# Batches 0 and 1 share the first layer by halves of its columns, and 1/sqrt is cut in two

## The chip, the core and the metric

The kernel runs on one core of a Trainium2 chip. The metric is the device time of one execution in microseconds (us); three runs of the kernel before gave a median of 1693.56 us (1692.34 to 1693.83). TensorE (PE) multiplies matrices, VectorE (DVE), ScalarE (ACT) and GpSimd (POOL) do elementwise work, and SyncE (SP) issues most DMAs. Every engine works through its own list of instructions in order; semaphores make one engine wait for another.

## The reference, cut to what matters

```
phi_w = softmax(phi, axis=seq) ; k_m = phi_w^T k ; v_m = phi_w^T v      # 8 batches, 8 heads, 576 tokens, 32 memories
x  = softmax(q k_m^T / 8) v_m                                            # -> 4608 tokens x 512
xn = x / sqrt(mean(x*x) + 1e-6) * rms_g
y  = (silu(xn @ w_gate) * (xn @ w_val)) @ w_out                          # 512 -> 1536 -> 512, float64 weights
out = (relu(y @ w_in2) ** 2) @ w_out2                                    # 512 -> 2048 -> 512
```

The weights arrive as 64-bit floats. The kernel turns each 128x512 piece of them into float32 on the core by integer work (a *conversion*), and splits every factor of the big products into a high and a low part, so that three matmuls make one product.

## The kernel before, in words

**Phase A** computes attention and the first layer (gate, val, out). A batch has 576 tokens, worked on in two halves of 288. The first layer's 1536 columns are cut into NF1 = 12 groups of 128. One *item* is one half of a batch's tokens with one column group: `phase_a` runs six matmuls for g (L748 to L750), Silu on ACT (L786), six matmuls for v, the product `sl` on DVE (L790), its high part `uh` on ACT and low part `ul` on POOL (the helper `split`, L68 and L72), and two items later twelve matmuls into the four accumulators y (`mm_out`, L762 to L764). A batch has 24 items, item n belongs to batch n // 24; there are 192. After the last column group of a half, y goes to `st` and by DMA to DRAM (L769 to L772). **Phase B** then runs the second layer from DRAM.

Into these items other work is put at four places, "a" to "d": after g, after v, after `split`, after `mm_out`. A table in `make_plan` says at which item of batch b which step of the attention of batch b+1 ("n") or b+2 ("p") is issued, and `slot` calls it. Steps that the prediction names: `p1` to `p7` (softmax of phi), `t1`, `a3` (k_m and v_m), `a7` to `a9` (scores), `a10` to `a15` (softmax), `a18`, `a19` and `sq_add` (x and its squares), `a20` (their sum), `a21` (1/sqrt by nine DVE operations, L467 to L475), `a23`, `an_split` (high and low part of x for the matmuls). The weights gate and val are folded with each batch's v_m: `wp_mm` (L504, PE) and `wp_ev` make the factors `wph`, `wpl` for two column groups at once, a *chunk*; there are six.

**Conversions.** `conv_next` starts one conversion (two ACT operations, L102 and L103) and ends the one started before: two DVE operations (L111, L112), an integer add on POOL (L116), for a piece of w_out ("o") also the high part `woh` on ACT and the low part `wol` on POOL, and then the next raw DMA (`next_raw`, four buffers). The first layer needs 36 conversions: 24 of gate and val ("g", "v", four for each chunk) and 12 of "o". The prologue, which computes batch 0's attention, calls `conv_next` five times; then `slot` calls it three times in each of items 0 to 11, since batch 0 takes the column groups in order and needs a new chunk every second item:

```
        if b == 0 and i < NF1 and pos in "abc":
            self.conv_next()
```

In PSUM there are one buffer for g, one for v, two for attention and four for y. The tiles of the items (`st`, `sl`, `uh`, `ul`) lie in a pool `up` that lives to the end.

Of the kernel before, what the change touches and what calls it, by code (L numbers as in the profile page):

```python
# [20 lines left out]
P = 128  # L21
# [15 lines left out]
NB1 = 6  # L37
# [16 lines left out]
class Kernel:  # L54
# [67 lines left out]
    def run(self):  # L122
# [3 lines left out]
        self.up = ctx.enter_context(self.pool("up"))  # L126
# [9 lines left out]
        self.idle = const.tile([P, 256], BF16, name="idle")  # L136
        nc.vector.memset(self.idle, 0.0)
# [5 lines left out]
        wa = self.pool("wa")  # L143
        self.wa = wa.__enter__()
# [17 lines left out]
        with tc.manual_schedule():  # L162
            self.phase_a(NI * (B - 1) + 3, NI * B + 2)
        wa.__exit__(None, None, None)
        self.wb2 = ctx.enter_context(tc.tile_pool(name="wb2", bufs=1, reuse_waits="tile"))
        with tc.manual_schedule():
            self.phase_b()
# [390 lines left out]
    def make_plan(self):  # L558
        self.early, self.warm_ps = 0, None
        self.w1, self.wo, self.wph, self.wpl, self.anh, self.anl = {}, {}, {}, {}, {}, {}  # L560
        keys = []
        for ch in range(NCH):
            keys += [(kind, ch, cp) for kind in "gv" for cp in range(2)]
            if ch:
                keys += [("o", 2 * ch - 2, 0), ("o", 2 * ch - 1, 0)]
        keys += [("o", NF1 - 2, 0), ("o", NF1 - 1, 0)]
# [4 lines left out]
        plan = [  # L571
            (0, "d", "b", "an_split", 1),
            (1, "a", "n", "a7", 0),
            (1, "a", "n", "load_q", 2),
            (1, "d", "n", "t1"),
            (1, "d", "n", "a3", 0),
            (2, "a", "n", "a7", 1),
            (2, "a", "n", "load_q", 3),
            (2, "b", "n", "a2"),
            (2, "c", "n", "a3", 1),  # L580
            (2, "d", "n", "a4"),
            (2, "d", "p", "load_phi"),
# [24 lines left out]
            (15, "a", "n", "a15", 1),
            (15, "b", "n", "a18", 0, 0),
            (15, "c", "n", "a19", 0, 0),
            (15, "d", "n", "a18", 0, 1),  # L610
            (15, "d", "n", "a19", 0, 1),
            (16, "c", "n", "sq_add", 0),
            (16, "c", "p", "p7"),
            (17, "b", "n", "a18", 1, 0),
            (17, "c", "n", "a19", 1, 0),
            (17, "d", "n", "a18", 1, 1),
            (17, "d", "n", "a19", 1, 1),
            (18, "c", "n", "sq_add", 1),
            (19, "b", "n", "a20", 0),
            (19, "c", "n", "a21", 0),  # L620
            (20, "c", "n", "a23", 0),
            (20, "d", "n", "an_split", 0),
            (21, "b", "n", "a20", 1),
            (21, "c", "n", "a21", 1),
            (22, "c", "n", "a23", 1),
        ]
        for ch in range(NCH):
            i = 14 + 2 * ch
            plan.append((i - 3, "d", "n", "wst_load", ch))
            if i < NI:  # L630
                plan += [(i, "a", "n", "wp_mm", ch), (i, "b", "n", "wp_ev", ch)]
            else:
                plan += [(i - NI, "a", "b", "wp_mm", ch), (i - NI, "b", "b", "wp_ev", ch)]
        self.plan = {}
        for i, pos, who, step, *args in plan:
            self.plan.setdefault((i, pos), []).append((who, step, args))

    def slot(self, b, i, pos):
        if b >= B:
            return  # L640
        for who, step, args in self.plan.get((i, pos), ()):
            n = {"b": b, "n": b + 1, "p": b + 2}[who]
            if n >= B or (b == 0 and who == "b" and step in ("wp_mm", "wp_ev")):
                continue
            getattr(self, step)(n, *args)
        if b == 0 and pos == "c" and i in (1, 3, 5, 7, 9):
            self.wp_mm(0, (i + 1) // 2)
            self.wp_ev(0, (i + 1) // 2)
        if b == 0 and i < NF1 and pos in "abc":
            self.conv_next()  # L650
        if 0 < b < B - 1 and i % 4 == 3 and i != NF1 - 1 and pos == "b":
            self.conv_next()
# [9 lines left out]
    def prologue(self):  # L662
# [51 lines left out]
        self.conv_next()  # L714
        self.p1(1)
# [16 lines left out]
        self.p6(1)  # L732
        self.a21(0, 1)
        self.a23(0, 1)
        self.p7(1)
        self.load_kv(1, 0)
# [15 lines left out]
    def mm_out(self, i):  # L752
        nc = self.nc
        hf, f = divmod(i % NI, NF1)
        if f == 0:
            self.y = [self.ps.tile([P, T], F32, tag=f"y{c}", name=f"y{i}_{c}") for c in range(KC)]
        hi, lo = self.wo[f]
        uh, ul = self.us.pop(i)
        for c in range(KC):
            cs = slice(c * P, (c + 1) * P)  # L760
            y = self.y[c][:, 0:HALF]
            nc.tensor.matmul(y, hi[:, cs], uh, start=(f == 0), stop=False)  # L762
            nc.tensor.matmul(y, lo[:, cs], uh, start=False, stop=False)  # L763
            nc.tensor.matmul(y, hi[:, cs], ul, start=False, stop=(f == NF1 - 1))  # L764
        if f == NF1 - 1:
            st = self.up.tile([P, KC, HALF], F32, tag="st", name=f"ys{i}")
            for c in range(KC):
                if c % 2:
# [3 lines left out]
            nc.sync.dma_start(self.y1[i // NF1], st)  # L772

    def phase_a(self, first, end):
        nc = self.nc
        if not first:
            self.us = {}
        for n in range(first, end):
            b, i = divmod(n, NI)
            hf, f = divmod(i, NF1)  # L780
            if b < B:
                gp = self.ps.tile([P, T], F32, tag="g", name=f"g{n}")[:, 0:HALF]
                self.mm_in(gp, b, hf, f, 0)
                self.slot(b, i, "a")
                sl = self.up.tile([P, T], F32, tag="sl", bufs=2, name=f"sl{n}")[:, 0:HALF]
# [3 lines left out]
                self.slot(b, i, "b")  # L789
                nc.vector.tensor_tensor(sl, sl, vp, op=ALU.mult)  # L790
                uh = self.up.tile([P, T], F32R, tag="uh", bufs=3, name=f"uh{n}")[:, 0:HALF]
                ul = self.up.tile([P, T], F32R, tag="ul", bufs=3, name=f"ul{n}")[:, 0:HALF]
                self.split(uh, ul, sl, lo_engine="pool")
                self.us[n] = (uh, ul)
                self.slot(b, i, "c")

            for m in () if f == 1 else (n - 2, n - 1) if f == 0 else (n - 2,):
                if m >= 0:
                    self.mm_out(m)
            self.slot(b, i, "d")  # L800
            if b == B - 1:
                if i >= 3:
                    self.w2_next(NF2)
# [152 lines left out]
```

## Time and profile before

| what | us |
|---|---|
| median of three runs | 1693.56 |
| the profiled execution | 1692.43 |
| its span, first to last instruction | 1690.6 |
| PE busy in the span | 1604.9 (95%) |
| DVE, ACT, POOL busy | 754.8, 605.4, 360.8 |

In the page's 40 slices PE is at 9 tenths or more from the sixth slice on (about 211 us); the first five show 6, 5, 7, 6 and 8 tenths with a granted clock of 8, 5, 7, 7 and 8 tenths of full speed. A matmul's duration in the rows is modelled with its overlap, so the number of matmuls in a stretch says more than the mean duration of one. "Idle before" a group of instructions names what ended that idle time.

### The profile page before, as it was taken

What the parts mean: (1) busy time and instruction counts of PE and PEld (TensorE: products, weight loads), DVE (VectorE), ACT (ScalarE), POOL (GpSimd) and SP (SyncE); (2) the same over time, 40 slices, a digit from 0 to 9 for tenths busy, and PEclk for the clock granted to TensorE, in tenths of its full rate; (3) what the DMA queues carried; (4) which work ended last, traced back from release to release, by engine and by line L of the source; (5) the groups of instructions that cost most, each with busy time, mean ns of one, the idle gap of its engine ahead of it and who ended that gap; (6) DMA issues with size and microseconds to landing.
All of it is one profiled execution on the core that took longest, in us unless ns stands there. A gap on an engine that the chain in (4) does not pass through costs nothing.

```text
span 1690.6 us, 25176 instructions
## 1 busy us (share of the span) xinstructions
PE 1604.9 (95%) x10206; PEld 1346.0 (80%) x10206; DVE 754.8 (45%) x1256; ACT 605.4 (36%) x1190; POOL 360.8 (21%) x384
## 2 busy tenths in 40 slices
PE   6576899999999999999999999999999999999998
PEld 3354688897988889798998888888888888888886
DVE  5878464646546564635444232323232323232322
ACT  2455534434353444434444222322232222232222
POOL 1466433434343343434220000000000000000000
PEclk8577899999999999999999999999999999999999
DMA  9697545474726546424323010101010101010000
GB/s 255 197 301 243 190 132 167 156 196 177 220 110 208 177 140 185 156 87 146 95 78 120 1 50 1 50 1 50 0 51 0 50 1 48 3 45 6 19 7 25
DMA packets 100293, 175.19 MB, mean 104 GB/s; under 512 B 23376, under 2 KB 65360, under 8 KB 94032
## 3 DMA queue, kind: packets, MB, share of 16 engines
q1 hardware_dynamic: 96592, 170.69, 32.3%
q10 hardware_dynamic: 3584, 2.88, 0.7%
q8 instruction: 80, 1.31, 0.3%
q14 instruction: 37, 0.30, 0.1%
HBM read 139.99 MB, written 33.55 MB: 103 GB/s over the span
## 4 chain that ended last, share of the span: by engine, by line
PE 81%; DVE 10%; ACT 3%; issue 2%; DMA 2%; POOL 1%; SPq 0%; ACTq 0%; DVEq 0%; POOLq 0%
PE z L898 8%; PE z L896 8%; PE h L858 8%; PE h L859 8%; PE h L857 8%; PE z L897 8%; PE y L762 5%; PE y L764 4%; PE y L763 4%; PE v L748 3%; PE g L748 3%; PE v L750 2%; PE v L749 2%; PE g L749 2%; PE wp L504 2%
## 5 line engine op out<-in xcount | busy, mean ns | idle before, releaser
L868 DVE TENSOR_TENSOR r<-r,h 128x512 f32<-128x512 f32 x144 | 99.0, 687 | 449.6 <-ACT r L867 449.3
L867 ACT ACTIVATE r<-h 128x512 f32<-128x512 f32 x144 | 86.1, 598 | 468.6 <-PE h L859 468.6
L72 POOL TENSOR_TENSOR ul<-sl,uh 128x288 fp32r<-128x288 f32 x192 | 160.4, 836 | 402.3 <-ACT uh L68 399.1
L762 PE MATMUL y<-uh,woh 128*128 128x288 f32 x768 | 237.2, 309 | 0.0
L896 PE MATMUL z<-bzh,gh 128*128 128x512 f32 x576 | 226.9, 394 | 1.4 <-ACT gh L68 1.4
L764 PE MATMUL y<-ul,woh 128*128 128x288 f32 x768 | 228.2, 297 | 0.0
L763 PE MATMUL y<-uh,wol 128*128 128x288 f32 x768 | 228.1, 297 | 0.0
L898 PE MATMUL z<-bzh,gl 128*128 128x512 f32 x576 | 226.5, 393 | 0.0
L858 PE MATMUL h<-xl,bih 128*128 128x512 f32 x576 | 224.9, 390 | 0.0
L859 PE MATMUL h<-xh,bil 128*128 128x512 f32 x576 | 224.5, 390 | 0.0
L857 PE MATMUL h<-xh,bih 128*128 128x512 f32 x576 | 224.3, 389 | 0.0
L897 PE MATMUL z<-bzl,gh 128*128 128x512 f32 x576 | 224.2, 389 | 0.0
L790 DVE TENSOR_TENSOR sl<-sl,v 128x288 f32<-128x288 f32 x192 | 86.1, 448 | 191.8 <-PE v L750 141.8
L762 PEld LDWEIGHTS y<-uh,woh 128*128 128x128 f32 x768 | 146.9, 191 | 20.6 <-issue 19.9
L68 ACT ACTIVATE uh<-sl 128x288 fp32r<-128x288 f32 x192 | 85.2, 444 | 179.5 <-DVE sl L790 178.8
L763 PEld LDWEIGHTS y<-uh,wol 128*128 128x128 f32 x768 | 147.1, 191 | 0.8
L764 PEld LDWEIGHTS y<-ul,woh 128*128 128x128 f32 x768 | 146.8, 191 | 0.0
L72 DVE TENSOR_TENSOR gl<-r,gh 128x512 fp32r<-128x512 f32 x144 | 99.8, 693 | 100.7 <-ACT gh L68 100.7
L786 ACT ACTIVATE sl<-g 128x288 f32<-128x288 f32 x192 | 78.3, 408 | 172.6 <-PE g L750 172.1
L748 PE MATMUL v<-anh,wph 128*128 128x288 f32 x384 | 121.9, 317 | 15.6 <-DVE sl L790 15.0
L748 PE MATMUL g<-anh,wph 128*128 128x288 f32 x384 | 119.8, 312 | 17.6 <-ACT sl L786 17.2
L68 ACT ACTIVATE gh<-r 128x512 fp32r<-128x512 f32 x144 | 91.1, 632 | 108.9 <-DVE r L868 108.9
(138 smaller groups left out, 2790.9 us busy)
## 6 DMA issues: line engine op xcount, KB each, us to landing
w<-w SPq DMA_DIRECT2D x48, 1024.0 KB
q<-in_q_dram SPq DMA_DIRECT2D x128, 144.0 KB
y<-ys SPq DMA_DIRECT2D x16, 576.0 KB
raw_i<-in_moe_w_in_dram SPq DMA_DIRECT2D x16, 512.0 KB
raw_z<-in_moe_w_out_dram SPq DMA_DIRECT2D x16, 512.0 KB
kv<-in_k_dram SPq DMA_DIRECT2D x14, 512.0 KB
kv<-in_v_dram SPq DMA_DIRECT2D x14, 512.0 KB
out_dram<-os SPq DMA_DIRECT2D x28, 256.0 KB
```

Source lines behind the costliest of these rows:

```text
L68: nc.scalar.activation(hi, src, AF.Copy)
L72: eng.tensor_tensor(lo, src, hi.bitcast(F32), op=ALU.subtract)
L748: nc.tensor.matmul(out, wh[:, r, cs], ah[:, r], start=(r == 0), stop=False)
L762: nc.tensor.matmul(y, hi[:, cs], uh, start=(f == 0), stop=False)
L763: nc.tensor.matmul(y, lo[:, cs], uh, start=False, stop=False)
L764: nc.tensor.matmul(y, hi[:, cs], ul, start=False, stop=(f == NF1 - 1))
L857: nc.tensor.matmul(hp, ih[:, cs], self.xh[c], start=(c == 0), stop=False)
L858: nc.tensor.matmul(hp, ih[:, cs], self.xl[c], start=False, stop=False)
L859: nc.tensor.matmul(hp, il[:, cs], self.xh[c], start=False, stop=(c == KC - 1))
L896: nc.tensor.matmul(y[c], gh[:, cs], oh, start=(f == 0), stop=False)
L897: nc.tensor.matmul(y[c], gh[:, cs], ol, start=False, stop=False)
L898: nc.tensor.matmul(y[c], gl[:, cs], oh, start=False, stop=(f == NF2 - 1))
```

## The change: what it does

1. **Order of the items.** A list `items` now says what item n is. Items 0 to 5 are column groups 0 to 5 of the first half of batch 0's tokens, 6 to 11 the same of its second half, 12 to 23 the same of batch 1; items 24 to 47 are column groups 6 to 11 in the same order. From item 48 on everything stands as before. So chunks 3 to 5 are first used at item 24, and batch 1's x is needed at item 12.
2. **y in two parts.** The sums over groups 0 to 5 of the two batches go to DRAM; at items 27, 33, 39 and 45 they are loaded again, and DVE adds the second part to them.
3. **Conversions.** Nine calls of `conv_next` stand in the prologue (five before), two in each of items 0 to 5, one in each of items 6 to 9 and 12 to 23. The order of the pieces changes too: chunks 0 and 1, "o" 0 and 1, chunk 2, "o" 2 to 11, chunks 3 to 5. In batches 1 to 6 there is one call more per batch.
4. **The table.** Batch 1's attention, in items 0 to 20 before, stands in items 0 to 11 (its second half of tokens to item 14); batch 2's phi steps stand in items 12 to 24. Batch 0's chunks 1 to 5 are folded at items 1, 3, 17, 21, 25, batch 1's at 9, 10, 12, 32, 34, 36. From batch 1's items on, `a21` is issued in two parts in successive items (nine DVE operations as five and four), and some steps shift by an item or two. The second `an_split` of batch 0 moves from item 0 into the prologue.
5. **Memory.** `anh`, `anl` get two buffers, the pool `up` ends with phase A, `sl`, `uh`, `ul` are 288 wide, and the idle matmuls of the prologue read `ones` in place of a tile of zeros.

```
+        for fs in (range(NF1 // 2), range(NF1 // 2, NF1)):
+            groups += [(b, hf, fs) for b in range(2) for hf in range(2)]
+        groups += [(b, hf, range(NF1)) for b in range(2, B) for hf in range(2)]
+        self.items = [(b, hf, f, f == fs[0], f == fs[-1]) for b, hf, fs in groups for f in fs]
...
+        keys = gv(0) + gv(1) + o(0, 1) + gv(2) + o(2, 3, 4, 5, 6, 7, 8, 9, 10, 11) + gv(3) + gv(4) + gv(5)
...
+            (10, "a", "a20", 0),
+            (10, "b", "a21", 0),
...
+        for n, ch in ((1, 1), (3, 2), (17, 3), (21, 4), (25, 5)):
+            at(n, "c", "wp_mm", 0, ch)
+            at(n, "c", "wp_ev", 0, ch)
...
+            (19, "c", 0, "a21", 0, 0),
+            (20, "c", 0, "a21", 0, 1),
...
+    def slot(self, n, pos):
+        for step, args in self.plan.get((n, pos), ()):
+            getattr(self, step)(*args)
+        if n < 6:
+            if pos in "ac":
+                self.conv_next()
+        elif n < 10 or NF1 <= n < NI:
+            if pos == "c":
+                self.conv_next()
+        elif NI <= n < NI * (B - 1) and pos == "b" and n % 4 == 3 and n % NI != NF1 - 1:
             self.conv_next()
+        elif NI <= n < NI * (B - 1) and pos == "c" and n % NI == NF1 + 1:
             self.conv_next()
...
+            st = self.st.pop("y", None)
+            add = st is not None
...
+                if add:
+                    nc.vector.tensor_tensor(st[:, c], st[:, c], self.y[c][:, 0:HALF], op=ALU.add)
...
+            if NI <= n < 2 * NI and n % 6 == 3:
+                t = self.up.tile([P, KC, HALF], F32, tag="st", name=f"yl{n}")
+                nc.sync.dma_start(t, self.y1[2 * b + hf])
+                self.st["y"] = t
```

ACT's list ahead of the first Silu, before (`sl0` is item 0's Silu, `cv_` and `cr_` the start of a conversion, `woh0` the high part of w_out's piece 0):

```order
L275 ACTIVATE ph1_311<-ph1_311 64x8x32
L102 ACTIVATE cv_g11_604<-raw_g1_1_371 128x512
L103 ACTIVATE cr_g11_605<-raw_g1_1_371 128x512
L786 ACT_TABLE_LOAD
L786 ACTIVATE sl0_614<-g0_597 128x288
```

and now (line numbers of the changed kernel; L67 is the high part of `split`, L895 the Silu):

```order
L274 ACTIVATE ph1_309<-ph1_309 64x8x32
L101 ACTIVATE cv_v10_581<-raw_v1_0_436 128x512
L102 ACTIVATE cr_v10_582<-raw_v1_0_436 128x512
L101 ACTIVATE cv_v11_601<-raw_v1_1_460 128x512
L102 ACTIVATE cr_v11_602<-raw_v1_1_460 128x512
L101 ACTIVATE cv_o00_613<-raw_o0_0_470 128x512
L102 ACTIVATE cr_o00_614<-raw_o0_0_470 128x512
L67 ACTIVATE anh0_1_623<-an0_0_443 128x288
L67 ACTIVATE anh0_1_623<-an0_1_450 128x288
L101 ACTIVATE cv_o10_653<-raw_o1_0_588 128x512
L102 ACTIVATE cr_o10_654<-raw_o1_0_588 128x512
L67 ACTIVATE woh0_660<-cv_o00_613 128x512
```

The first Silu now stands behind three further starts of conversions, behind the second half of batch 0's x and behind `woh0`, which needs POOL's add of w_out's piece 0.

DVE's list between the products `sl43` and `sl45` of items 43 and 45, before (`sqt2` and `sq2_1` are the nine operations of batch 2's 1/sqrt):

```order
L790 TENSOR_TENSOR sl43_3145<-sl43_3145,v43_3147 128x288
L467 TENSOR_SCALAR sqt2_2955<-ss2_0_3154 128x288
L468 TENSOR_SCALAR sq2_1_2954<-sqt2_2955 128x288
L469 TENSOR_TENSOR sqt2_2955<-sq2_1_2954 128x288
L470 TENSOR_TENSOR sqt2_2955<-sqt2_2955 128x288
L471 TENSOR_SCALAR sqt2_2955<-sqt2_2955 128x288
L472 SCALAR_TENSOR_TENSOR sqt2_2955<-sqt2_2955 128x288
L473 SCALAR_TENSOR_TENSOR sqt2_2955<-sqt2_2955 128x288
L474 SCALAR_TENSOR_TENSOR sqt2_2955<-sqt2_2955 128x288
L475 SCALAR_TENSOR_TENSOR sq2_1_2954<-sqt2_2955,sq2_1_2954 128x288
L72 TENSOR_TENSOR wpl2_3_3221<-wp2_3_0_3201,wph2_3_3220 128x512
L72 TENSOR_TENSOR wpl2_3_3221<-wp2_3_1_3202,wph2_3_3220 128x512
```

and now:

```order
L899 TENSOR_TENSOR sl43_3164<-sl43_3164,v43_3166 128x288
L467 TENSOR_SCALAR sqt2_2955<-ss2_0_3173 128x288
L468 TENSOR_SCALAR sq2_1_2954<-sqt2_2955 128x288
L469 TENSOR_TENSOR sqt2_2955<-sq2_1_2954 128x288
L470 TENSOR_TENSOR sqt2_2955<-sqt2_2955 128x288
L471 TENSOR_SCALAR sqt2_2955<-sqt2_2955 128x288
L71 TENSOR_TENSOR wpl2_3_3224<-wp2_3_0_3204,wph2_3_3223 128x512
L71 TENSOR_TENSOR wpl2_3_3224<-wp2_3_1_3205,wph2_3_3223 128x512
L899 TENSOR_TENSOR sl44_3214<-sl44_3214,v44_3216 128x288
L474 SCALAR_TENSOR_TENSOR sqt2_2955<-sqt2_2955 128x288
L475 SCALAR_TENSOR_TENSOR sqt2_2955<-sqt2_2955 128x288
L476 SCALAR_TENSOR_TENSOR sqt2_2955<-sqt2_2955 128x288
```

Item 44's product now has five operations of the 1/sqrt ahead of it where it had nine; the other four follow it.

## Rows read from the trace of the kernel before

**Rows 1.** Windows: stretch and length, engines' busy us (instructions), clock, DMA share, GB/s.
```profile
62.10:186.60 124.50, 79.07 (x492) 58.89 (x492) 97.46 (x119) 69.68 (x126) 79.69 (x64) 0.70 0.79 250
186.60:234.10 47.50, 46.78 (x381) 38.55 (x384) 29.19 (x56) 19.54 (x47) 18.62 (x22) 0.96 0.37 134
234.10:330.90 96.80, 95.00 (x840) 83.04 (x842) 54.24 (x101) 42.62 (x93) 37.79 (x42) 1.00 0.53 166
330.90:427.80 96.90, 95.07 (x841) 83.09 (x847) 54.28 (x101) 42.61 (x93) 38.94 (x44) 1.00 0.55 174
```

**Rows 2.** Timeline of ACT: Silu of items 0, 12, 24 and 48.
```profile
62.18 0.41 ACT L786 ACTIVATE sl<-g 128x288 f32<-128x288 f32 x1
...
186.71 0.41 ACT L786 ACTIVATE sl<-g 128x288 f32<-128x288 f32 x1
...
234.23 0.41 ACT L786 ACTIVATE sl<-g 128x288 f32<-128x288 f32 x1 [1.43 <-PE g L750]
...
331.02 0.41 ACT L786 ACTIVATE sl<-g 128x288 f32<-128x288 f32 x1 [0.32 <-PE g L750]
```

**Rows 3.** Windows, line 112 alone (DVE): busy us (instructions), clock, DMA.
```profile
62.10:186.60 124.50, 45.50 (x36) 0.70 0.79 250
...
330.90:427.80 96.90, 3.46 (x5) 1.00 0.55 174
```

**Rows 4.** Windows, line 111 alone (DVE).
```profile
62.10:186.60 124.50, 28.07 (x36) 0.70 0.79 250
```

**Rows 5.** Windows, line 116 alone (POOL).
```profile
62.10:186.60 124.50, 48.61 (x36) 0.70 0.79 250
...
330.90:427.80 96.90, 6.69 (x6) 1.00 0.55 174
```

**Rows 6.** Waits of PE and ACT from 62.1 to 186.6: us, times, longest.
```profile
PE g L748 <- ACT sl L786: 11.7, 5, 4.4
PE wp L504 <- POOL w L116: 10.2, 5, 3.0
PE v L748 <- DVE sl L790: 8.0, 4, 4.9
...
ACT woh L68 <- POOL cv_o L116: 21.6, 12, 3.0
```

**Rows 7.** Groups by line, POOL, 62.17 to 186.6: busy us, mean ns | idle before.
```profile
L72 POOL TENSOR_TENSOR wol<-cv_o,woh 128x512 fp32r<-128x512 f32 x12 | 15.6, 1300 | 8.9 <-ACT woh L68 8.9
...
L72 POOL TENSOR_TENSOR ul<-sl,uh 128x288 fp32r<-128x288 f32 x12 | 11.0, 920 | 1.0 <-ACT uh L68 1.0
```

**Rows 8.** Timeline of the prologue's end: start us, us, engine, operation [idle before].
```profile
19.05 0.61 PE L293 MATMUL t<-ones,es 128*128 128x2 f32 x4
...
54.12 0.81 ACT L68 ACTIVATE anh<-an 128x288 fp32r<-128x288 f32 x2 [5.37 <-DVE an L482]
...
60.88 1.28 ACT L786 ACT_TABLE_LOAD   x1
...
75.71 1.63 DVE L112 SCALAR_TENSOR_TENSOR cv_o<-raw_o,cv_o 128x512 uint32<-128x512 uint32 x1
...
78.78 0.63 ACT L68 ACTIVATE woh<-cv_o 128x512 fp32r<-128x512 f32 x1 [1.28 <-POOL cv_o L116]
```

**Rows 9.** Windows, line 504 alone (PE, folding of the weights).
```profile
330.90:427.80 96.90, 6.56 (x104) 1.11 (x111) 1.00 0.55 174
```

**Rows 10.** Waits of PE from 330.9 to 427.8.
```profile
PE v L748 <- DVE sl L790: 1.5, 2, 1.3
```

**Rows 11.** Timeline around that wait: DVE's 1/sqrt, the product, PE's next matmul.
```profile
407.88 0.46 DVE L467 TENSOR_SCALAR sqt<-ss 128x288 f32<-128x288 f32 x1
...
412.35 0.46 DVE L472 SCALAR_TENSOR_TENSOR sqt<-sqt 128x288 f32<-128x288 f32 x1
...
415.40 0.44 DVE L790 TENSOR_TENSOR sl<-sl,v 128x288 f32<-128x288 f32 x1
...
415.90 0.40 PE L748 MATMUL v<-anh,wph 128*128 128x288 f32 x1 [1.30 <-DVE sl L790]
```

More of the change, by code (lines that the diff above doesn't have):

```diff
@@ L36 @@
 NI = 2 * NF1
-NB1 = 6
 EPS = 1e-9
@@ L628, in make_plan @@
             i = 14 + 2 * ch
[L629 to L649, printed above, removed]
+            steps += [(i - 3, "d", 0, "wst_load", ch), (i, "a", 0, "wp_mm", ch), (i, "b", 0, "wp_ev", ch)]
+        for b in range(1, B - 1):
+            for i, pos, ahead, step, *args in steps:
+                at(NI * b + i, pos, step, b + 1 + ahead, *args)
+    def slot(self, n, pos):
[8 more added lines that the diff above has]
+        elif NI <= n < NI * (B - 1) and pos == "b" and n % 4 == 3 and n % NI != NF1 - 1:
             self.conv_next()
-        if 0 < b < B - 1 and i % 4 == 3 and i != NF1 - 1 and pos == "b":
+        elif NI <= n < NI * (B - 1) and pos == "c" and n % NI == NF1 + 1:
             self.conv_next()
@@ L714, in prologue @@
         self.conv_next()
+        self.conv_next()
         self.p1(1)
@@ L750, in mm_in, with mm_out @@
             nc.tensor.matmul(out, wl[:, r, cs], ah[:, r], start=False, stop=(r == NR - 1))
-    def mm_out(self, i):
+    def mm_out(self, n):
         nc = self.nc
-        hf, f = divmod(i % NI, NF1)
-        if f == 0:
-            self.y = [self.ps.tile([P, T], F32, tag=f"y{c}", name=f"y{i}_{c}") for c in range(KC)]
+        b, hf, f, first, last = self.items[n]
+        if first:
+            self.y = [self.ps.tile([P, T], F32, tag=f"y{c}", name=f"y{n}_{c}") for c in range(KC)]
         hi, lo = self.wo[f]
-        uh, ul = self.us.pop(i)
+        uh, ul = self.us.pop(n)
         for c in range(KC):
@@ L761, in mm_out @@
             y = self.y[c][:, 0:HALF]
[L762 removed]
+            nc.tensor.matmul(y, hi[:, cs], uh, start=first, stop=False)
             nc.tensor.matmul(y, lo[:, cs], uh, start=False, stop=False)
[L764 to L766 removed]
+            nc.tensor.matmul(y, hi[:, cs], ul, start=False, stop=last)
+        if last:
+            st = self.st.pop("y", None)
+            add = st is not None
+            if not add:
+                st = self.up.tile([P, KC, HALF], F32, tag="st", name=f"ys{n}")
             for c in range(KC):
[L768 removed]
+                if add:
+                    nc.vector.tensor_tensor(st[:, c], st[:, c], self.y[c][:, 0:HALF], op=ALU.add)
+                elif c % 2:
                     nc.vector.tensor_copy(st[:, c], self.y[c][:, 0:HALF])
@@ L771, in mm_out, with phase_a @@
                     nc.scalar.activation(st[:, c], self.y[c][:, 0:HALF], AF.Copy)
-            nc.sync.dma_start(self.y1[i // NF1], st)
-    def phase_a(self, first, end):
+            nc.sync.dma_start(self.y1[2 * b + hf], st)
+    def phase_a(self, start, end):
         nc = self.nc
-        if not first:
+        if not start:
             self.us = {}
[L778 to L781, printed above, removed]
+        for n in range(start, end):
+            first = True
+            if n < len(self.items):
+                b, hf, f, first, _ = self.items[n]
                 gp = self.ps.tile([P, T], F32, tag="g", name=f"g{n}")[:, 0:HALF]
                 self.mm_in(gp, b, hf, f, 0)
-                self.slot(b, i, "a")
-                sl = self.up.tile([P, T], F32, tag="sl", bufs=2, name=f"sl{n}")[:, 0:HALF]
+                self.slot(n, "a")
+                sl = self.up.tile([P, HALF], F32, tag="sl", bufs=2, name=f"sl{n}")
                 nc.scalar.activation(sl, gp, AF.Silu)
```

255 lines of the change are left out of this document (171 added, 84 removed).

## The prediction

> **What bounds the kernel now.** I read the page's 40 slices first, then the windows cut at the items' Silus, then the waits inside the bad stretch. The page has PE at 9 tenths from the sixth slice on; nearly all that can be won lies ahead of that. The Silus of items 0, 12, 24 and 48 start at 62.2, 186.7, 234.2 and 331.0 us [rows 2]. A batch in the middle takes 96.9 us with PE busy for 95.1 [rows 1], so 4.0 us an item and PE the bound. Items 12 to 23 take 47.5 us, the same pace. Items 0 to 11 take 124.5 us, 10.4 an item, at a mean granted clock of 0.70, that is, part of the time at 1.2 GHz and part at 2.4. DVE is busy for 97.5 us there (78%), POOL for 79.7 (64%), PE for 79.1.
>
> These twelve items hold all but a few of the conversions: 36 of them end there [rows 3 to 5]. One takes on DVE (45.50 + 28.07) / 36 = 2.04 us, and 48.61 / 36 = 1.35 on POOL; line 112 alone takes 1.26 there and 3.46 / 5 = 0.69 in a quiet batch. PE waits in order for what stands behind them: Silu behind ACT's starts, the fold behind POOL's add, v's next matmul behind the product [rows 6]. ACT itself sits 21.6 us, 1.8 for each of twelve "o" pieces, waiting for POOL's add.
>
> **The change part by part.**
>
> *Conversions.* At item 0's Silu, 9 stand behind us on DVE in the new order (4 before). Items 0 to 9 end 15, items 12 to 23 end 12. So the first twelve items lose 21 of 36, but only one of twelve "o".
>
> *Item 0's Silu comes later.* It stood behind little; now it stands behind `woh0`, and that behind DVE's ninth conversion. The same DVE work, in nearly the same order, reaches that point before at 75.7 (start of line 112), and `woh0` at 78.78 [rows 8]. So: 78.8 + 0.6 for it, less 0.4 for item 0's product, which no longer stands among them, plus the table load of 1.28 [rows 8]: 80.2 us, against 62.2. Nothing is lost by that alone, since the conversions are done then. If the five conversions of this piece ran without the 0.57 that line 112 gains (1.26 - 0.69), it would be 77.3. If POOL's low part of the second half came in between, 2.2 more. I keep 80.2.
>
> *Items 0 to 11.* DVE: 15 x 2.04 = 30.6; the rest was 97.5 - 73.6 = 23.9; in come one 1/sqrt (6.3 us, from 407.9 to 414.2 [rows 11]) and the last softmax steps (some 4), out go two phi steps (some 4). That is 60.8. At DVE's share of 78% it makes 78 us. POOL: 15 x 1.35 = 20.3, eleven `wol` of 1.30, twelve `ul` of 0.92 [rows 7], and batch 1's attention, 38.9 - 6.7 - 24 x 0.92 = 10.1 [rows 1, 5, 7]: 55.8, at its share of 64% 87 us. PE as the bound below: the order has 373 matmul instructions there, a middle batch 706 in 96.9 us, so 51 us. The upper end is the 124.5 of before. I take 86, near POOL's figure, since the "o" pieces, for which ACT sits, have not become fewer.
>
> *Items 12 to 23.* PE has 317 matmul instructions against 346 in 47.5 us: about 45. Twelve conversions are new: DVE 29.2 + 12 x 2.04, less some 9 of the attention that has left, is about 45 too, so it is close. I take 49: three long pieces of DVE (1/sqrt, two phi steps) for which PE waits 1.3 us each, as it does for one now [rows 10]. Ends: 45 and, at the 0.70 clock, 45 / 0.70 = 64.
>
> *Items 24 to 47.* 96.8 us, and three folds of weights more, 3 x 6.56 / 6 = 3.3 [rows 9], less the wait of 1.3 that goes with the split (below): 98.8. The loads of y have from three items ahead (over 10 us) and DVE's adds lie in an item where no `mm_out` follows at once: cost nothing; with that cover gone, four more DVE operations of about 0.45 a group, 4 x 0.9 = 3.6 in all. kv of batch 1 is now queued behind four more raw pieces and wanted one item sooner; 2.3 MB at 250 GB/s [rows 1] is 9 us, covered by the 18 by which the first Silu is late; uncovered, 9. Two more table loads on ACT, at items 23 and 24, cost 2 x 1.28 [rows 8] on an engine busy for 44% of a middle batch: nothing. The Trainium skill ("ScalarE: Activation LUTs", Table sets) puts a switch of sets at about 2.7 us; the trace has 1.28, and the trace decides.
>
> *1/sqrt in two, batches 2 to 7.* PE's one wait of 1.3 us in a batch [rows 10] is for the product that stands behind nine operations and two low parts, from 407.9 to 415.4 [rows 11]. Four of the nine (412.35 to 414.2, 1.8 us) now come after it, so the wait goes: 1.3 in each of batches 1 to 6, of which the five from item 48 on are 6.5. What is late next is the product itself behind the same two low parts, which no longer reach PE. Ends: 0, if the second part delays another product as much, and 8.
>
> *Phase B* reads the same things from other places: 0. The tiles that lie under its first ones were last read by items before the end.
>
> *Sum.* Item 48's Silu: 80.2 + 86 + 49 + 98.8 = 314.0, against 331.0: -17.0; with -6.5: -23.5. The profiled execution took 1692.4; 1668.9 there. The median is 1.1 higher: 1670.
>
> **The rivals.**
>
> *PE becomes the bound early.* Fewer conversions keep PE busy, the clock stays at 2.4 GHz, and the stretches take 77, 51, 45 and 98: 271 at item 48, -60 and -6.5: 1627. For it: PE at 95% as soon as conversions end, at 186.6 [rows 1]. Against it: eleven "o" pieces remain, and POOL needs 55.8 us itself. Between this and the forecast, with 78 for the Silu, 68 for items 0 to 11 and 46 for 12 to 23, lies 1647 (291 at item 48).
>
> Line 112 takes 1.26 us beside a busy POOL and 0.69 beside an idle one [rows 3]. By the Trainium skill ("SBUF — State Buffer", Who interferes with whom) DVE's operations with two inputs in SBUF and GpSimd's share one pair of ports, taken for a whole instruction. By that rule their times add: before 79.7 + 36 x 0.69 = 104.5 of 124.5 us, then 55.8 + 15 x 0.69 + some 4 for the 1/sqrt = 70, and items 0 to 11 could not take 51 us, only 70 (1646 in all); the trace agrees by the 1.26.
>
> *Slower: batch 1's attention doesn't fit into twelve items.* It is one chain of some 19 hand-overs between engines, each waited for in order by PE, DVE or POOL. Batch 0's took 54.1 - 19.05 = 35 us in the prologue [rows 8], with little else in the queues. If each hand-over now waits behind a whole "o" conversion (2.04 on DVE, 1.35 + 1.30 on POOL, 4.7), it takes 35 + 89 = 124 us, the first twelve items as long as before, and the kernel 1670 + 38 = 1708. It decides from 35 + 19 x 3.9 = 109.5 on, where the 23.5 are gone. Against it: items 5 to 9 have one conversion each and 10 and 11 none, and a usual wait is half of a conversion: 35 + 45 = 80, under the 86.
>
> *It doesn't do what it says.* The conversions are only moved: one per item is enough to keep PE at 0.70 in items 12 to 23 (64 in place of 49), and items 0 to 11 take 4 more than I took: +19, 1689. For it: DVE's and PE's loads there are both about 45 of 49. Against: before, with three conversions an item, PE still got 0.70.
>
> **How the numbers follow.** Forecast 1670 (own range 1655 to 1682) 0.50; the way to PE's bound, 1647, 0.18; PE's bound itself, 1627, 0.08; conversions only moved, 1689, 0.15; slower, 1708, 0.09. From no change (0.2% of the median is 3.4 us, about what a measurement here can tell) 1689 is hardly apart: a third of its chance counts as the same. Faster 0.86, the same 0.05, slower 0.09. For 8 in 10 the range leaves out the two outer cases: 1638 to 1692.
>
> **What would show it.** In the new profile: item 0's Silu near 80, item 12's near 166, item 24's near 215, item 48's near 314. Line 112's mean still over 1.0 us up to item 10 and its count about 15 between items 0 and 12. No wait of v for the product over 0.5 us in a batch from the third on, and a middle batch near 95.6 us. A granted clock of 1.00 from item 12 on. I am wrong if PE waits for the chain of batch 1 (for `an`, `kvz`, `qt` or `anh`) for more than 15 us in items 0 to 12, if the first Silu is past 90, or if phase B starts with a wait.

## The result and the profile after

The changed kernel takes 1706.3 us (median of four runs, 1702.9 to 1707.8), against 1693.0 for the kernel before on the same chip: 1.0077 of it [1.0059, 1.0094]. It is slower by 13, and 36 above the forecast of 1670. Its profiled execution took 1702.94 us, with a span of 1701.1.

The Silus of items 0, 12, 24 and 48 of the changed kernel, from the timeline of ACT; these rows answer to [rows 2]:

```profile
78.89 0.41 ACT L895 ACTIVATE sl<-g 128x288 f32<-128x288 f32 x1
...
175.71 0.41 ACT L895 ACTIVATE sl<-g 128x288 f32<-128x288 f32 x1 [0.72 <-PE g L853]
...
233.70 0.41 ACT L895 ACTIVATE sl<-g 128x288 f32<-128x288 f32 x1
...
343.21 0.39 ACT L895 ACTIVATE sl<-g 128x288 f32<-128x288 f32 x1
```

The windows between them, and the two batches after (columns as in [rows 1]):

```profile
78.80:175.60 96.80, 67.55 (x478) 50.29 (x483) 48.75 (x84) 45.72 (x91) 53.66 (x49) 0.76 0.56 176
175.60:233.60 58.00, 52.04 (x375) 48.15 (x374) 36.93 (x62) 32.73 (x64) 31.47 (x29) 0.91 0.80 240
233.60:343.10 109.50, 99.58 (x869) 82.33 (x867) 65.72 (x120) 44.85 (x98) 37.16 (x41) 0.97 0.65 223
343.10:439.00 95.90, 94.75 (x837) 83.56 (x832) 59.45 (x106) 42.91 (x94) 41.12 (x45) 1.00 0.58 184
439.00:535.30 96.30, 95.28 (x840) 83.59 (x834) 58.74 (x104) 43.48 (x96) 41.10 (x45) 1.00 0.58 183
```

| us | before | forecast | after |
|---|---|---|---|
| item 0's Silu | 62.2 | 80.2 | 78.9 |
| items 0 to 11 | 124.5 | 86 | 96.8 |
| items 12 to 23 | 47.5 | 49 | 58.0 |
| items 24 to 47 | 96.8 | 98.8 | 109.5 |
| item 48's Silu | 331.0 | 314.0 | 343.2 |
| batches 2 to 6 together | 481.2 | 474.7 | 478.5 |

So the time is lost in four places, by 11, 9, 11 and 4 us against the forecast; less the 1.3 by which item 0's Silu is early, that is 33 of the 34 us between the forecast for the profiled execution (1668.9) and its time. In the first window DVE is busy for 50% and POOL for 55%, where before they had 78% and 64%, and PE for 70%: no engine is full there. What PE waits for in it (us, times, longest), which answers to [rows 6]:

```profile
PE g L851 <- ACT sl L895: 15.8, 5, 6.2
PE kv L315 <- ACT woh L67: 12.1, 1, 12.1
PE sc L371 <- DVE wpl L71: 2.7, 1, 2.7
PE ss L456 <- ACT sq L443: 2.2, 1, 2.2
PE x L427 <- DVE an L416: 1.9, 2, 1.2
```

and ACT:

```profile
ACT woh L67 <- POOL cv_o L115: 21.5, 11, 2.8
```

The timeline between the Silus of items 4 and 5 shows how the two hang together. DVE's two conversion steps, POOL's add, ACT's `woh`, POOL's `wol`, and the next add follow one another, and Silu stands behind `woh`:

```profile
121.21 1.27 POOL L115 TENSOR_TENSOR cv_o<-cv_o,cr_o 128x512 int32<-128x512 int32 x1 [1.09 <-DVE cv_o L111]
...
122.52 0.63 ACT L67 ACTIVATE woh<-cv_o 128x512 fp32r<-128x512 f32 x1 [2.15 <-POOL cv_o L115]
...
123.22 1.41 POOL L71 TENSOR_TENSOR wol<-cv_o,woh 128x512 fp32r<-128x512 f32 x1 [0.74 <-ACT woh L67]
...
124.60 1.15 POOL L393 TENSOR_TENSOR L<-L,lm 128x576 f32<-128x576 f32 x1
125.71 1.25 POOL L115 TENSOR_TENSOR cv_o<-cv_o,cr_o 128x512 int32<-128x512 int32 x1
127.00 0.63 ACT L67 ACTIVATE woh<-cv_o 128x512 fp32r<-128x512 f32 x1 [2.73 <-POOL cv_o L115]
127.53 0.39 ACT L895 ACTIVATE sl<-g 128x288 f32<-128x288 f32 x1
127.70 1.28 POOL L71 TENSOR_TENSOR wol<-cv_o,woh 128x512 fp32r<-128x512 f32 x1 [0.74 <-ACT woh L67]
127.96 0.46 DVE L899 TENSOR_TENSOR sl<-sl,v 128x288 f32<-128x288 f32 x1 [3.80 <-ACT sl L895]
```

ACT idles, then POOL idles, then DVE: a ring of hand-overs, each engine half empty. PE's longest wait for Silu, 6.2 us, ends with item 5's Silu here. Not all of the 15.8 us are this ring. The 3.6 us of item 2 lie behind a start of a conversion for which ACT waits for a transfer:

```profile
99.22 0.66 ACT L101 ACTIVATE cv_v<-raw_v 128x512 f32<-128x512 f32 x1 [3.97 <-DMA raw_v<-in_moe_w_val_dram]
...
100.78 0.40 PE L851 MATMUL g<-anh,wph 128*128 128x288 f32 x1 [3.60 <-ACT sl L895]
```

Ahead of item 6's Silu, ACT has batch 1's softmax (two operations) with a table load of 1.28 us on either side, after `woh`.

### The profile page after: what moved, and what is told of

Its sections match the earlier page's. It is cut to its first block, busy times and chain, and to the rows that moved or that the text cites. A ratio compares the mean times of both kernels' runs of the same rounds, so it can differ in the third digit from the quotient of the medians.

```text
span 1701.1 us, 25184 instructions
## 1 busy us (share of the span) xinstructions
PE 1604.4 (94%) x10206; PEld 1349.1 (79%) x10206; DVE 758.3 (45%) x1271; ACT 605.7 (36%) x1192; POOL 365.1 (21%) x384
## 4 chain that ended last, share of the span: by engine, by line
PE 82%; DVE 7%; DMA 4%; ACT 3%; issue 2%; POOL 2%; SPq 0%; ACTq 0%; DVEq 0%; POOLq 0%
PE h L973 8%; PE h L971 8%; PE h L972 8%; PE z L1011 8%; PE z L1012 8%; PE z L1010 8%; PE y L865 5%; PE y L866 5%; PE y L867 5%; PE v L851 3%; PE g L851 3%; PE v L852 2%; PE v L853 2%; PE g L852 2%; PE g L853 2%; PE wp L506 2%
## 5 line engine op out<-in xcount | busy, mean ns | idle before, releaser
L71 POOL TENSOR_TENSOR ul<-sl,uh 128x288 fp32r<-128x288 f32 x192 | 166.4, 867 | 384.8 <-ACT uh L67 383.0
L67 ACT ACTIVATE uh<-sl 128x288 fp32r<-128x288 f32 x192 | 85.2, 444 | 193.2 <-DVE sl L899 193.2
L895 ACT ACTIVATE sl<-g 128x288 f32<-128x288 f32 x192 | 78.4, 408 | 166.2 <-PE g L853 163.0
L67 ACT ACTIVATE gh<-r 128x512 fp32r<-128x512 f32 x144 | 91.0, 632 | 108.8 <-DVE r L982 108.8
```

Source lines behind the costliest of these rows:

```text
L67: nc.scalar.activation(hi, src, AF.Copy)
L71: eng.tensor_tensor(lo, src, hi.bitcast(F32), op=ALU.subtract)
```

## The experiments

"Mending" below means an edit to the changed kernel unless it says otherwise. The kernel before ran beside every group of runs, with medians of 1693.0 to 1693.8.

**1. w_out's parts one call later.** The high and low part of a w_out piece are issued at the end of the next `conv_end`, when POOL's add has long been done.

```
+        if self.late:
+            f0, t0 = self.late.pop()
+            (hi, lo of t0; wo[f0])
         if kind == "o":
-            (hi, lo of t; wo[f])
+            self.late.append((f, t))
```

> The changed kernel with the high and low part of each w_out piece taken one conversion call later, so that ACT no longer stands behind POOL's add just ahead of the next Silu. Theory 1 (the w_out pieces set the pace of items 2 to 9): ACT's 21.5 us of waiting for POOL's add go, items 2 to 9 shrink by 10 to 16 us, the kernel is near 1692 to 1696. Theory 2 (batch 1's attention chain sets the pace of items 0 to 11): under 3 us, 1703 to 1706. Theory 3 (late transfers): under 3 us.

1692.9 us, 13.4 less than the changed kernel (0.9997 of before [0.9984, 1.0011]). Items 0 to 11 fall to 89.0, PE's wait for Silu from 15.8 to 10.6. The pieces did set part of the pace. Two thirds of PE's wait stay, and of ACT's 21.5 us for POOL's add half comes back in another form: 7.4 + 3.4 us in which the start of the next conversion waits for `wol`, the low part.

**2. The same edit to the kernel before.**

> The kernel before, with the later split of the w_out pieces alone. Theory 1: the pieces also hold back items 0 to 11 there (ACT waits 21.6 us for them), 8 to 12 us faster, 1681 to 1685. If DVE's and POOL's load (78% and 64%) set the pace there: under 3 us.

1693.3 (0.9995 [0.9986, 1.0005]): nothing. This fits the second theory, that with 36 conversions in the same items DVE and POOL were the bound, but it doesn't settle it: here ACT's wait was hardly removed, since 13.8 + 4.6 us of waiting for `wol` came in place of the 21.6 for POOL's add.

**3. Batch 1's k and v earlier.** `load_kv(1, ...)` stands ahead of the last five calls of `conv_next` in the prologue, not behind them.

```
+        self.load_kv(1, 0)
+        self.load_kv(1, 1)
         self.conv_next()
         self.conv_next()
         self.p1(1)
...
         self.an_split(0, 1)
-        self.load_kv(1, 0)
-        self.load_kv(1, 1)
```

> The changed kernel with batch 1's keys and values loaded ahead of the last raw weights of the prologue. Theory 3 (late transfers): PE's 12.1 us in front of a3 shrink to 7 and item 1's Silu comes 5 us sooner, the kernel 1701. Theory 1: the same 5 us at first, of which the w_out pieces that follow take most back: 1703 to 1706. Theory 2: 5 us, since the chain begins sooner.

1697.9 (1.0018 [1.0009, 1.0028]), 8.3 less, more than any of the three theories had; PE's wait of 12.1 for `kv` is gone, and items 0 to 11 fall from 96.8 to 89.4. That wait was for a transfer, whatever releaser the row names: the changed kernel issues the loads from 74.51 to 82.4 us (SP's and PE's timeline).

```profile
74.51 1.13 SPq L187 DMA_DIRECT2D kv<-in_k_dram  x1
...
84.36 2.52 PE L315 MATMUL kv<-kv,ph 128*32 128x128 f32 x40 [12.13 <-ACT woh L67]
```

The kernel before issued them from 45.76 us on:

```profile
45.76 0.94 SPq L188 DMA_DIRECT2D kv<-in_k_dram  x1
```

In between stand raw pieces, further ahead in SP's queue, which wait for conversions to free their buffers. The longest of SP's waits from 35 to 84 us:

```profile
SPq L81 <- DVE cv_g L111: 15.0, 1, 15.0
```

**4. The folds.** Chunk 5 is folded at item 24, not 25; batch 1's chunks 3 and 4 are loaded at items 22 and 26, not 28 and 31.

```
-            (28, "d", "wst_load", 3),
-            (31, "d", "wst_load", 4),
+            (22, "d", "wst_load", 3),
+            (26, "d", "wst_load", 4),
...
-        for n, ch in ((1, 1), (3, 2), (17, 3), (21, 4), (25, 5)):
+        for n, ch in ((1, 1), (3, 2), (17, 3), (21, 4), (24, 5)):
```

> The changed kernel with batch 0's last chunk folded at item 24 in place of 25, and batch 1's chunks 3 and 4 loaded at items 22 and 26 in place of 28 and 31. If items 24 to 47 are 12.7 us longer than before because PE waits for two attention buffers (3.5 us ahead of t1) and for the fourth chunk's load (3.9 us): both waits go, items 24 to 47 take 101 to 103 us, the kernel 1698 to 1700. If DVE's load there (65.7 against 54.2 us) is the reason, the waits come back elsewhere: 1704 to 1706.

1697.0 (1.0017 [1.0007, 1.0026]), 9.3 less by the medians; in the profiles items 24 to 47 take 105.6 in place of 109.5, where 101 to 103 were expected. PE's waits there, in the changed kernel:

```profile
PE wp L506 <- DMA w<-w: 3.9, 1, 3.9
PE t L292 <- DVE wpl L71: 3.5, 1, 3.5
PE v L851 <- DVE sl L899: 2.2, 1, 2.2
```

and with the mending:

```profile
PE t L292 <- DVE es L285: 2.8, 1, 2.8
...
PE wp L506 <- DMA w<-w: 1.1, 1, 1.1
```

The load now comes 1.1 us late and not 3.9. `t` no longer waits for the two PSUM buffers that chunk 5 held, but for the next thing, `p7`'s result.

**5. The 1/sqrt alone.** The kernel before with `a21` in two parts, in items 19 to 22.

```
-            (19, "c", "n", "a21", 0),
-            (20, "c", "n", "a23", 0),
+            (19, "c", "n", "a21", 0, 0),
+            (20, "c", "n", "a21", 0, 1),
+            (21, "a", "n", "a23", 0),
...
-            (21, "c", "n", "a21", 1),
-            (22, "c", "n", "a23", 1),
+            (21, "c", "n", "a21", 1, 0),
+            (22, "c", "n", "a21", 1, 1),
+            (23, "c", "n", "a23", 1),
```

> The kernel before with nothing but the 1/sqrt of batches 1 to 7 issued in two parts (five and four operations, in successive items, the second half's too). By the step of the prediction, a wait of 1.3 us goes in each batch from 0 on: some 8 us less, 1685.5, and no wait of v for the product above 0.5 us in a middle batch. The rival: the changed kernel's middle batches were only 0.5 to 1.0 us shorter and its wait of v for sl still 1.0; then the split is worth 0.5 a batch, 3 to 4 us in all, 1690. A third: nothing, 1693 to 1694, because the second part delays another product as much.

1682.9 (0.9936 [0.9925, 0.9948]): 10.5 less, somewhat more than forecast. A middle batch takes 95.0, and PE's waits in one (519.9 to 614.8) are all in this row; the wait of [rows 10] is gone:

```profile
PE g L753 <- ACT sl L791: 0.3, 1, 0.3
```

So the changed kernel, with the same split and 96.3 us for such a batch, loses 1.3 a batch elsewhere.

**6. Three mendings together** (1, 3 and 4).

> The changed kernel with three mendings at once: the high and low parts of a w_out piece issued one conversion later, batch 1's k and v loaded ahead of the last raw pieces of the prologue, chunk 5 folded an item earlier and batch 1's chunks 3 and 4 loaded 5 to 6 items earlier. If the three costs lie behind one another (places: items 2 to 9, item 0 to 2, items 25 to 47), the gains add: 1706.3 - 13.4 - 8.3 - 9.3 = 1675, item 48's Silu near 316. The rival: the waits cover each other (PE waits for the k and v of batch 1 while the w_out pieces run through anyway), and the sum is no more than some 20: 1686, Silu of 48 at 326.

1680.4 (0.9926 [0.9913, 0.9939]). Of 31.0 added up, 25.9 remain: nearer to places one behind another than to cover. Items 0 to 11 take 84.3.

**7. Six w_out pieces out of items 4 to 9** into items 12 to 23.

```
-keys = ... + o(2, ..., 11) + gv(3) + gv(4) + gv(5)
+keys = ... + o(2, 3, 4, 5) + gv(3) + o(6, 7) + gv(4) + o(8, 9) + gv(5) + o(10, 11)
...
-        if n < 6:
+        if n < 4 or NF1 <= n < NI and n % 2:
             if pos in "ac":
                 self.conv_next()
-        elif n < 10 or NF1 <= n < NI:
+        elif n < 6 or NF1 <= n < NI:
```

> The changed kernel with the last six w_out pieces, first needed at item 26, moved out of items 4 to 9 into items 12 to 23, among the pieces of chunks 3 to 5 (there three conversions every two items, none in items 6 to 11). If w_out pieces pace items 2 to 9, items 0 to 11 fall from 96.8 to 80 to 87 us, and if items 12 to 23 are not bound by load (DVE 37, POOL 31 of 58 us busy) they stay within 3 us of 58: 1692 to 1699. The rival, that the conversions' time is only moved: items 12 to 23 grow by what items 0 to 11 win, 1703 to 1708.

1710.1 (1.0109 [1.0087, 1.0131]): slower still. Items 0 to 11 fall to 83.8 as the first theory had it, but items 12 to 23 rise to 79.7 (the profiled execution took 1719.9, the longest of the four and 10 above their median). PE's wait for Silu in items 0 to 11, and then in 12 to 23:

```profile
PE g L851 <- ACT sl L895: 1.9, 1, 1.9
...
PE g L851 <- ACT sl L895: 19.2, 5, 6.3
```

In the changed kernel these are 15.8 and 3.8. The wait goes where the pieces go, though DVE and POOL are no busier in items 12 to 23 than there (64% and 56% now; 64% and 54%). It is not the number of w_out pieces alone: five are left in items 0 to 11, with 1.9 us. And items 12 to 23 also have six conversions more, so the run doesn't tell w_out pieces from conversions as such; its rival, that time is only moved, fits it.

**8. The same with the three mendings.**

> The three mendings together with the last six w_out pieces in items 12 to 23. If both the place of the w_out split and the number of pieces in items 2 to 9 matter, it beats the three mendings alone by 3 to 8 us: 1667 to 1672. If the late split already took the w_out pieces off the path, no difference or, with 18 conversions in items 12 to 23 in place of 12, some us slower: 1675 to 1680.

1686.7 (0.9963 [0.9950, 0.9975]), worse than without the spreading and than either expectation. (The last piece ahead of item 6 is split in item 6, since no conversion follows it there.) Items 0 to 11 fall from 84.3 to 73.2, items 12 to 23 rise from 58.7 to 72.0, with 13.0 us of PE's wait for Silu, though the split comes a call late. So further conversions, with their transfers, cost time there, and not the ring alone.

**9. The seventh conversion of a batch.** The change put one more `conv_next` into item 13 of each of batches 1 to 6. Six more conversions are not needed; two are, and these stand in batch 6.

```
-        elif NI <= n < NI * (B - 1) and pos == "c" and n % NI == NF1 + 1:
+        elif pos == "c" and n in (NI * (B - 2) + 5, NI * (B - 2) + 9):
```

> The changed kernel with one edit: the seventh conversion of batches 1 to 6 (ended in item 13 of the batch, ahead of the softmax sums, the fold's low part and the product of that item) goes; the two of them that are still needed stand in batch 6, items 5 and 9. Theory: this conversion gives back what the 1/sqrt in two parts wins, since its two DVE operations took 1.30 and 1.17 us beside POOL's add in the changed kernel and item 13 takes 2.79 us there against 1.63, item 15 5.27 against 4.85: 1.2 to 1.6 in each of six batches, so 7 to 10 us, 1696 to 1699, middle batches near 95.0 and PE's wait of v for sl of 1.0 gone. Rival: another edit of the table holds the middle batches at 96.4: 1704 to 1707.

1692.6 (0.9992 [0.9983, 1.0001]), 13.7 less by the medians. Batches 2 to 6 take 472.4 in place of 478.5, and from 435.9 to 530.7, a middle batch, PE has no wait at all; the changed kernel has one of 1.0. Its timeline around that conversion:

```profile
490.65 1.16 POOL L408 TENSOR_TENSOR L<-L,ls 128x576 f32<-128x576 f32 x1 [0.62 <-DVE ls L407]
...
490.80 1.30 DVE L110 TENSOR_SCALAR cv_i<-cv_i 128x512 uint32<-128x512 uint32 x1
...
491.77 0.99 POOL L71 TENSOR_TENSOR ul<-sl,uh 128x288 fp32r<-128x288 f32 x1
...
492.13 1.17 DVE L111 SCALAR_TENSOR_TENSOR cv_i<-raw_i,cv_i 128x512 uint32<-128x512 uint32 x1
...
494.92 1.22 DVE L71 TENSOR_TENSOR wpl<-wp,wph 128x512 fp32r<-128x512 f32 x2
...
496.06 0.44 DVE L899 TENSOR_TENSOR sl<-sl,v 128x288 f32<-128x288 f32 x1
...
496.56 0.40 PE L851 MATMUL v<-anh,wph 128*128 128x288 f32 x1 [1.01 <-DVE sl L899]
```

PE's matmul stands behind the product, and that behind two softmax sums, the fold's low part and this conversion of 2.47 us. The same two operations in run 5's kernel, in item 14, beside an idle POOL:

```profile
481.99 0.38 DVE L111 TENSOR_SCALAR cv_i<-cv_i 128x512 uint32<-128x512 uint32 x1
482.41 0.69 DVE L112 SCALAR_TENSOR_TENSOR cv_i<-raw_i,cv_i 128x512 uint32<-128x512 uint32 x1
```

**10 and 11. All of it.** Mendings 6 and 9; batch 1's chunks 0 and 1 loaded two items earlier, its second 1/sqrt in two parts, `p6` and `p7` of batch 2 an item earlier. In the second of the two, the parts of a w_out piece are issued at the start of the next call, not at its end.

```
-            (7, "a", "wst_load", 0),
+            (5, "b", "wst_load", 0),
...
-            (13, "c", "a21", 1),
+            (13, "c", "a21", 1, 0),
+            (14, "c", "a21", 1, 1),
...
-            (24, "a", "p6"),
-            (24, "d", "p7"),
+            (23, "c", "p6"),
+            (24, "a", "p7"),
```

> The three mendings together (1680.4 measured) with the conversion moved, batch 1's chunks 0 and 1 loaded two items earlier, the 1/sqrt of batch 1's second half in two parts, and the two phi steps p6 and p7 of batch 2 an item earlier. By the waits left in the profile of the three mendings: 7 to 10 us from the conversion, 2.8 from PE's wait of t for es, 2.1 from v for sl in items 12 to 23, up to 3.5 of the fold's wait in items 0 to 11: 1664 to 1671. If only the conversion counts: 1671 to 1674.

> The same, but the high and low part of a w_out piece are issued at the very start of the next call, ahead of the next piece's start on ACT and its add on POOL, not behind them. With the late split ACT waited 7.4 us in items 0 to 11 for a piece's buffer to come free of POOL's low part, and PE still 8.2 for Silu; if these come from the low part being behind the next add, items 0 to 11 lose 3 to 7 us: 1658 to 1667. If the high part now waits for POOL's add again, as in the changed kernel, it is slower: 1670 to 1680.

1664.4 (0.9834 [0.9821, 0.9847]) and 1664.1 (0.9824 [0.9811, 0.9837]): 29.4 and 29.7 us less than the kernel before, and no difference between the two. The windows of the second, by item 0, 12 and 24:

```profile
75.80:158.30 82.50, 65.74 (x438) 49.57 (x446) 51.68 (x84) 44.99 (x90) 57.07 (x51) 0.80 0.59 188
158.30:214.10 55.80, 50.66 (x377) 45.56 (x373) 39.78 (x64) 33.39 (x65) 31.82 (x28) 0.94 0.85 257
214.10:311.20 97.10, 95.74 (x857) 81.91 (x863) 60.86 (x116) 44.06 (x97) 35.95 (x40) 1.00 0.71 239
```

**12 to 14. Items 12 to 23.** In the changed kernel ACT waits there for a raw piece, and Silu behind it, and PE behind Silu (timeline of ACT and PE):

```profile
209.69 0.66 ACT L101 ACTIVATE cv_v<-raw_v 128x512 f32<-128x512 f32 x1 [2.95 <-DMA raw_v<-in_moe_w_val_dram]
...
211.38 0.42 ACT L895 ACTIVATE sl<-g 128x288 f32<-128x288 f32 x1
...
211.85 0.61 PE L851 MATMUL g<-anh,wph 128*128 128x288 f32 x1 [3.82 <-ACT sl L895]
```

Windows around it and around an earlier wait of 2.1 for a product (length, busy time of PE, PEld, DVE, ACT, POOL, then clock, DMA share, GB/s):

```profile
182.00:189.00 7.00, 4.89 (x36) 4.55 (x34) 6.16 (x14) 2.02 (x5) 1.19 (x2) 1.00 1.01 303
189.00:196.00 7.00, 6.98 (x41) 6.98 (x42) 6.93 (x9) 5.12 (x12) 5.54 (x6) 0.76 1.07 297
196.00:204.00 8.00, 8.00 (x65) 6.53 (x64) 4.68 (x8) 3.75 (x9) 5.81 (x6) 1.00 1.07 301
204.00:211.00 7.00, 4.03 (x31) 3.79 (x29) 4.42 (x8) 2.64 (x7) 3.19 (x3) 0.98 1.04 263
211.00:216.00 5.00, 4.15 (x18) 4.15 (x19) 1.71 (x4) 2.77 (x7) 2.41 (x2) 0.50 0.78 290
```

Run 12 loads batch 2's k, v and first two q columns at items 20 to 23, not 12 to 15; run 13 does so in the fastest kernel (run 11's); run 14 moves only k and v there. Run 12's edit:

```
-            (12, "d", "load_kv", 0),
-            (13, "d", "load_kv", 1),
-            (14, "d", "load_q", 0),
-            (15, "d", "load_q", 1),
...
+            (20, "d", "load_kv", 0),
+            (21, "d", "load_kv", 1),
+            (22, "d", "load_q", 0),
+            (23, "d", "load_q", 1),
```

> The changed kernel with one edit: batch 2's k, v and first two q columns are loaded at items 20 to 23 in place of 12 to 15. Theory: in items 12 to 23 of the changed kernel a raw piece stands in SP's queue behind these loads, ACT waits 2.9 us for it and 1.8 for another, Silu stands behind ACT's start of the conversion, PE waits 3.8 us for that Silu at 211.85 and the granted clock is 0.50 in the 5 us after. Then items 12 to 23 fall from 58.0 by 3.8 + 2.5 + some of the 1.2 others, to 50 to 53, and the kernel to 1699 to 1702, unless item 25 then waits for k and v. Rival: the wait is the order of the conversions on DVE and POOL, not the loads: items 12 to 23 stay within 2 us of 58 and the kernel at 1704 to 1708.

> The fastest so far (w_out parts issued first, 1664.1 measured) with the same move of batch 2's k, v and q loads to items 20 to 23. If the loads delay the raw pieces there too (items 12 to 23 take 55.8 us), it gains 3 to 6 us: 1658 to 1661. If batch 2's k and v then come late for item 25, items 24 to 35 give it back: 1664 to 1667.

> The fastest so far (1664.1) with only batch 2's k and v (2.3 MB) loaded at items 20 and 21; its q stays at items 14 and 15. In the runs with k, v and q moved, items 12 to 23 fell (58.0 to 52.3 in the changed kernel, 55.8 to 53.6 in the mended one) and items 24 to 35 gave back 5.6 and 13.2, as DVE's transpose of q at item 24 waited 4.55 us for q. If q alone was late, items 12 to 23 stay near 53 and items 24 to 35 near 48: 1660 to 1663. If k and v are late as well, 24 to 35 take 52 or more: 1665 to 1672.

1708.9 (1.0087 [1.0073, 1.0101]), 1672.7 (0.9870 [0.9857, 0.9884]) and 1665.5 (0.9830 [0.9816, 0.9844]). Each time items 12 to 23 fall (58.0 to 52.3, 55.8 to 53.6, 55.8 to 52.4), and no wait of ACT for a raw piece is left. Each time items 24 to 35 give it back (58.5 to 64.1, 48.0 to 61.2, 48.0 to 54.3). DVE then waits in its order, in run 12 for q and in run 14 for the first part of y:

```profile
237.04 0.78 DVE L359 STREAM_TRANSPOSE qt<-q 128x576 f32<-128x576 f32 x1 [4.55 <-DMA q<-in_q_dram]
```

```profile
242.63 1.55 DVE L880 TENSOR_TENSOR yl<-yl,y 128x288 f32<-128x288 f32 x4 [6.32 <-DMA yl<-y]
```

So the raw pieces' place behind those loads is the cause of 5.7 us in items 12 to 23 (run 12); that another order of the loads would be free is not shown.

## Why the prediction was wrong

**What held.** Item 0's Silu (80.2; 78.9). The conversions of items 0 to 11 became as few as forecast, 15. The 1/sqrt in two is worth its 8 us and more (run 5). The two more table loads take 1.28 each and cost PE 0.3 us at most. Of the signs that the prediction gave, four failed: line 111, which is line 112 of [rows 3], has 13.59 / 15 = 0.91 us in items 0 to 11, not over 1.0; v waits 1.0 us for a product in a middle batch, not under 0.5; the granted clock is 0.91 in items 12 to 23 and 0.97 in 24 to 47, not 1.00; and the Silus from item 12 on are late.

**The step that failed: items 0 to 11, 86 forecast and 96.8 measured.** The prediction took the work of DVE (60.8) and POOL (55.8) and divided by the shares of before, 78% and 64%. That left out what PE waits for in order while these engines are half empty. Two waits count:

- *ACT's wait for POOL's add.* It is 21.6 us for twelve pieces before [rows 6] and 21.5 for eleven now. The prediction named it and priced it only by choosing POOL's 87 over DVE's 78. Now Silu, and PE with it, stands behind a part of it: issued later, it gives back 7.8 us of items 0 to 11 (run 1).
- *k and v of batch 1.* They were "covered by the 18 by which the first Silu is late", so they had no price. They were not covered: with the raw pieces ahead in SP's queue their loads start 29 us later than before (run 3). Without that wait items 0 to 11 take 7.4 us less. The uncovered price was put at 9, and run 3 gains 8.3 in all.

With both mended items 0 to 11 take 84.3 (run 6), near the 86. That does not bear out the shares: DVE's work in the changed kernel is 48.8 us and not 60.8, since a conversion takes it (13.59 + 10.02) / 15 = 1.57 us and not 2.04, and 8.2 us of PE's wait for Silu are still in the 84.3. The rival on the slow side gave 1708, near the result, by luck: it had each hand-over of batch 1's attention behind a whole conversion, and PE waits for that chain only 2.7 + 2.2 + 1.9 us.

Two sums of the prediction are off without bearing on this: 317 / 346 of 47.5 us is 43.5, not about 45; and 3.6 us for the added parts of y is two more operations of 0.45 us for each of the four groups, not four. And by the trace's count of matmuls (478 in items 0 to 11, some 840 in a middle batch) PE's own bound there is 55 us, not 51.

**Items 12 to 23.** The forecast, 49 us, added 12 conversions on DVE and compared the engines' busy time. It left out their 12 transfers of 512 KB beside batch 2's k, v, phi and q, and by the windows the DMA engines are full there from 182 to 211 us (1.01 to 1.07). Run 12, without those loads, has 52.3. PE waits 3.8 us for Silu and 2.1 for a product behind batch 1's nine operations of 1/sqrt. After each of them the granted clock is lower: 0.50 in 211 to 216 us, 0.76 in 189 to 196, so part of the time at 1.2 GHz; ahead of the waits, with PE at work, it is 1.00. Over all of items 12 to 23 it is 0.91; if PE's work is stretched by as much, that is 58.0 x 0.09 = 5.2 us, an estimate, and with the waits 11.1, about what lies between the 47.5 of before and 58.0. So a wait of PE costs nearly twice its length here. It is not so of every wait: a middle batch of the kernel before has one of 1.3 us [rows 10] and a granted clock of 1.00 [rows 1].

**Items 24 to 47.** Only the folds' matmuls were priced (3.3). Their two PSUM buffers and their 1 MB loads, which stand in SP's queue behind q and y, cost 3.5 and 3.9 in waits. Run 4 gains 3.9 of the 10.7 us above the forecast. In runs 10 and 11, with `p6` and `p7` an item earlier and the seventh conversion gone as well, these items take 97.3 and 97.0, below it; which of the two brings how much was not run. That the loads of y cost nothing holds in the changed kernel; run 14 shows it hangs on what stands ahead of them.

**Batches 2 to 6.** The seventh conversion is in the text on the change, and got no price; it costs 478.5 - 472.4 = 6.1 us (run 9). A quiet conversion is 0.38 + 0.69 us of DVE (run 5's kernel); here it is 1.30 + 1.17, beside POOL's multiplication of the softmax (not its add, as the expectation had it) and `ul`, in the one item where DVE already has the softmax sums, the fold's low part and a product that PE needs. By the Trainium skill ("SBUF — State Buffer", Who interferes with whom), DVE and GpSimd share a pair of ports, and when a DVE operation is in its two-port mode the engine that issues first holds the pair for its whole instruction and blocks the other; one with two inputs in SBUF contends with GpSimd's reads. The rows agree: line 111, with two inputs, takes 1.17 beside `ul` and 0.69 without, and line 110, issued 0.15 us after POOL's multiplication, ends 0.29 us after it does, where 0.38 is its own length. Which mode line 110 runs in is not shown.

**What is left open.** The fastest kernel still takes 82.5 us for items 0 to 11, with 9.2 of PE's wait for Silu there. And the medians of runs 4 and 9 lie 9.3 and 13.7 under the changed kernel's, where the spans of the profiled executions (1694.9 and 1692.3) lie 6.2 and 8.8 under its 1701.1: that execution is the fastest of its four, so these gains are known to some 3 to 5 us only. How much of PE's wait for Silu in items 0 to 11 is w_out pieces and how much conversions as such stays open too (runs 7 and 8).

## What to carry to other kernels

When a change takes load from the bound, the old busy share doesn't say what comes next: look at the waits that lay beside the busy engines and price each of them. An operation that waits for another engine is better issued a step late than ahead of something that the bound engine waits for (run 1; it changed nothing in run 2). Count each added operation in the repeated part of a program, however small, at the place where it stands, and each transfer by what is ahead of it in its queue.

## What the runs showed of the hardware

The named releaser of PE's wait for `kv` was an ACT operation; the true one, a DMA, is seen only in SP's timeline, and a run of the same order (run 1) has the same 12.1 us put down to the DMA. And a part of what a wait of PE costs can come after it: the 5 us behind the 3.82 us wait had a granted clock of 0.50, 2.5 us more by estimate.
